# Half of a batch's feed-forward moved out of the attention stage, by way of DRAM, into Strassen's form

## The chip, the cores and the metric

The kernel runs on one core of one Trainium2 chip. Its engines are TensorE (PE in the profile; PEld is its weight load), VectorE (DVE), ScalarE (ACT), GpSimd (POOL) and SyncE (SP), which issues most of the DMAs. The metric is the device time in microseconds (us). Each engine works its own list of instructions, which is fixed when the program is built; a layer that plans the program sets the order in each list.

## The reference

Four batches of eight heads with 768 positions and a head dimension of 64. Queries and keys are each given to the nearest of 16 centroids of their head; a query sees the keys of its own cluster alone. The heads' results stand side by side as 3072 rows of 512 features, and these go through a feed-forward block: a product with `w_in` (512 x 2048), the square of the positive part, and a product with `w_out` (2048 x 512).

```python
q_assign = np.argmax(np.einsum('bhsd,hcd->bhsc', q_n, c_n), axis=-1)   # q_n, k_n, c_n: of length 1
k_assign = np.argmax(np.einsum('bhsd,hcd->bhsc', k_n, c_n), axis=-1)
mask = q_assign[:, :, :, None] == k_assign[:, :, None, :]
scores = np.where(mask, scale * np.matmul(q, k.transpose(0, 1, 3, 2)), -1000000000.0)
attn = np.exp(scores - np.max(scores, axis=-1, keepdims=True))
attn = attn / (np.sum(attn, axis=-1, keepdims=True) + 1e-09)
x = np.matmul(attn, v).transpose(0, 2, 1, 3).reshape(B * S, H * D)
r = np.maximum(x @ w_in, 0.0)
out = (r * r) @ w_out
```

The weights come as 64-bit numbers, which the kernel rounds to 32 bits itself.

## The kernel before

**Units.** Attention goes by pairs of heads (16 pairs, four to a batch) and by halves `h` of the 768 queries (384 columns, `TB`). One unit is one pair, one half and 256 of the 768 keys: 96 units, numbered 0 to 95 here; batch 0 has units 0 to 23, and each later pair has six units, three for `h` = 0 and three for `h` = 1.

**One unit of batches 1 to 3.** `scores` puts four products (two chunks of keys, two heads) into two PSUM tiles named `sc`, chunk 1 first. There are two such tiles (`ps_sc`), so the next unit's scores write the same two again. ScalarE takes the exponential in place, one instruction for each tile (line 466). VectorE reads the PSUM tile, sets to zero what belongs to another cluster, and writes an SBUF tile `ex` (line 470, four instructions a unit, here called masks; two for each `sc` tile). A tile of scores is free only when its two masks are done. `times_v` multiplies `ex` by the values two units later (`LAG = 2`), into `av`. GpSimd adds the `ex` tiles up for the sums (lines 480 and 482). In batch 0 the mask is part of the product instead, and ScalarE writes `ex` itself.

**The end of a half.** Three units after its first scores, the sums are spread by a product with ones (`sm`), VectorE takes the reciprocal `r` (line 551), which goes by SyncE to DRAM (`far_r`) and comes back to all partitions (`rb`); VectorE multiplies `av` by it into `xT` (line 570).

**The next pair.** Its queries and keys are turned by DMA (`qkT<-words`), multiplied by the centroids (`lg`), copied (`lgs`), transposed (`lt`), and VectorE finds the clusters in five instructions (`number`: `mx`, `best` twice, `ids`, `ids_b`). These numbers are turned (`pb`), copied (`row`), and go by way of DRAM to all partitions (`qid`).

**The fill.** Between these products TensorE works on the feed-forward of batch 0, in plain form: a generator `ffn(b, h)` yields after each product, and the loop over units takes as many columns from it as `density` and what is `left` ask for. `ffn` first makes 16 tiles `gT`, one for each 128 of the 2048 features (`ph`, line 584: 4 products of 384 columns each; ScalarE then does lines 591 and 592), and then three times 16 products of 512 columns (`po`, line 597). The fill uses the PSUM pool `ps_f` of two banks together with `sm`, `lg`, `lt` and `pb`.

**After attention.** For batches 1, 2, 3 in turn `ffn_pair` does the feed-forward in Strassen's form, with 7 products where the plain form has 8: first up (line 676, all of `g`, 16 x 2 x 384 columns for each partition), then down (line 707), in three column parts `i` of 128. `combine` adds the seven results up on VectorE (line 646 and `sub`, line 618). `w_sums` are the four sums of blocks of `w_out` (tiles `w_t`) that the down products need; they are made once.

A product of 32-bit numbers shows in the profile as two MATMUL records, so a unit has 8 records of `sc` and 8 of `av`.

Of the kernel before, what the change touches and what calls it, by code (L numbers as in the profile page):

```python
# [8 lines left out]
F32 = mybir.dt.float32  # L9
# [16 lines left out]
def kernel(  # L26
# [28 lines left out]

    outer, ctx, keep, early = ctx, ExitStack(), ExitStack(), ExitStack()
    xtp = keep.enter_context(tc.tile_pool(name="xtp", bufs=1))
    gtp = ctx.enter_context(tc.tile_pool(name="gtp", bufs=FT))
    xt_first = ctx.enter_context(tc.tile_pool(name="xt_first", bufs=1))
    loads = ctx.enter_context(tc.tile_pool(name="loads", bufs=4))  # L60
    loads_v = ctx.enter_context(tc.tile_pool(name="loads_v", bufs=2))
# [11 lines left out]
    once_early = early.enter_context(tc.tile_pool(name="once_early", bufs=1, side="right"))  # L73
    later = {}

    dram = ctx.enter_context(tc.tile_pool(name="dram", bufs=2, space=bass.MemoryType.DRAM))
    ps_sc = ctx.enter_context(tc.tile_pool(name="ps_sc", bufs=2, space=PSUM))
    ps_av = ctx.enter_context(tc.tile_pool(name="ps_av", bufs=2, space=PSUM))
# [496 lines left out]


    out_view = out.rearrange("(b p j) m -> b j p m", p=P, j=NCH)

    def ffn(b, h):
        gT = []  # L580
        for f in range(FT):
            ph = bank("ph", [P, TB])
            for kk in range(KT):
                nc.tensor.matmul(  # L584
                    ph, lhsT=w_in[:, kk, f * P : (f + 1) * P], rhs=xT[b, h][:, kk],
                    start=(kk == 0), stop=(kk == KT - 1),
                )
                if kk < KT - 1:
                    yield TB
            gT.append(gtp.tile([P, TB], F32, name="gT"))  # L590
            nc.scalar.activation(out=gT[f], in_=ph, func=ACT.Relu)
            nc.scalar.square(gT[f], gT[f])
            yield TB
        for i in range(NB):
            po = bank("po", [P, DM])
            for f in range(FT):
                nc.tensor.matmul(  # L597
                    po, lhsT=gT[f][:, i * P : (i + 1) * P], rhs=w_out[:, f],
                    start=(f == 0), stop=(f == FT - 1),
                )  # L600
                if f < FT - 1:
                    yield DM
            osb = later["out"].tile([P, DM], F32, name="osb")
            nc.scalar.copy(out=osb, in_=po)
            nc.sync.dma_start(out_view[b, h * NB + i], osb)
            yield DM

    def ffn_pair(pools, b):  # L610

        gp, sp, tp, bk = pools
        H2, F2, M2 = KT // 2, FT // 2, DM // 2
        x = [[xT[b, h][:, H2 * g : H2 * (g + 1)] for h in range(2)] for g in range(2)]
        t1, t2, t4 = (tp.tile([P, H2, TB], F32, name=f"x_t{i}") for i in (1, 2, 4))

        def sub(out, a, b, eng=nc.vector):
            eng.tensor_tensor(out=out, in0=a, in1=b, op=ALU.subtract)

        with tc.issue_after(last_exp[0]):  # L620
            sub(t1, x[0][1], x[0][0])
            sub(t2, x[1][1], t1)
            sub(t4, t2, x[1][0])
            sub(x[0][1], x[1][1], x[0][1])
        t3 = x[0][1]
        g = gp.tile([P, FT, 2, TB], F32, name="g")

        def combine(c, product, width, early=()):

            (c11, c12), (c21, c22) = c

            waiting = {}

            def bank_of(j):
                if j in waiting:
                    return waiting[j]
                bank = bk(width)
                product(j, bank)  # L640
                return bank

            def add(j, *results):
                bank = bank_of(j)
                for out, to in results:
                    nc.vector.tensor_tensor(out=out, in0=bank, in1=to, op=ALU.add)  # L646

            bank = bk(width)
            product(1, bank)
            nc.scalar.copy(out=c11, in_=bank)  # L650
            for j in early:
                waiting[j] = bank_of(j)
            add(6, (c12, c11))
            add(2, (c11, c11))
            add(7, (c21, c12))
            add(5, (c22, c21), (c12, c12))
            sub(c21, c21, bank_of(4))
            add(3, (c12, c12))

        for i in range(F2):  # L660
            lo, hi = slice(i * P, (i + 1) * P), slice((F2 + i) * P, (F2 + i + 1) * P)
            a = [[w_in[:, H2 * g2 : H2 * (g2 + 1), cols] for g2 in range(2)] for cols in (lo, hi)]
            w_s = sp.tile([P, 4, H2, P], F32, name="w_s", tag=f"s{i % 2 + 1}")
            s1, s2, s3, s4 = (w_s[:, j] for j in range(4))
            nc.gpsimd.tensor_tensor(out=s1, in0=a[1][0], in1=a[1][1], op=ALU.add)  # L665
            sub(s2, s1, a[0][0], nc.gpsimd)
            sub(s3, a[0][0], a[1][0], nc.gpsimd)
            sub(s4, a[0][1], s2, nc.gpsimd)
            operands = {
                1: (a[0][0], x[0][0]), 2: (a[0][1], x[1][0]), 3: (s4, x[1][1]), 4: (a[1][1], t4),  # L670
                5: (s1, t1), 6: (s2, t2), 7: (s3, t3),
            }

            def product(j, bank):
                for kk in range(H2):
                    nc.tensor.matmul(  # L676
                        bank, lhsT=operands[j][0][:, kk], rhs=operands[j][1][:, kk],
                        start=(kk == 0), stop=(kk == H2 - 1),
                    )

            if i > 1 and w_sums:
                to, one, two = w_sums.pop(0)
                sub(w_t[to], one, two)
            c = [[g[:, f, h] for h in range(2)] for f in (i, F2 + i)]
            combine(c, product, TB)
            nc.scalar.activation(out=c[0][0], in_=c[0][0], func=ACT.Relu)
            nc.scalar.square(c[0][0], c[0][0])
            for to in (c[1][1], c[1][0], c[0][1]):
                nc.vector.scalar_tensor_tensor(
                    out=to, in0=to, scalar=0.0, in1=to, op0=ALU.max, op1=ALU.mult  # L690
                )

        for i in range(NB):
            cols = slice(i * P, (i + 1) * P)
            a = [[g[:, F2 * g2 : F2 * (g2 + 1), h, cols] for g2 in range(2)] for h in range(2)]
            s1, s2 = (sp.tile([P, F2, P], F32, name=f"g_s{j}", tag=f"s{j}") for j in (1, 2))
            nc.vector.tensor_tensor(out=s1, in0=a[1][0], in1=a[1][1], op=ALU.add)
            sub(s2, s1, a[0][0])
            sub(a[1][0], a[0][0], a[1][0])
            operands = {  # L700
                1: (a[0][0], w_q[0][0]), 2: (a[0][1], w_q[1][0]), 3: (a[0][1], w_q[1][1]),
                4: (a[1][1], w_t[4]), 5: (s1, w_t[1]), 6: (s2, w_t[2]), 7: (a[1][0], w_t[3]),
            }

            def product(j, bank):
                for f in range(F2):
                    nc.tensor.matmul(  # L707
                        bank, lhsT=operands[j][0][:, f], rhs=operands[j][1][:, f],
                        start=(f == 0), stop=(f == F2 - 1),
                    )  # L710
                if j == 2:
                    sub(a[0][1], a[0][1], s2)

            osb = [later["out"].tile([P, DM], F32, name="osb") for _ in range(2)]
            c = [[osb[h][:, M2 * m : M2 * (m + 1)] for m in range(2)] for h in range(2)]
            last = b == B - 1 and i == NB - 1
            combine(c, product, M2, early=(2, 4))

            for h in (1, 0):
                for cols in (slice(0, M2), slice(M2, DM)) if last and h == 0 else (slice(0, DM),):  # L720
                    nc.sync.dma_start(out_view[b, h * NB + i][:, cols], osb[h][:, cols])


# [5 lines left out]
        for pair in pairs for h in halves for c in range(0, NCH, 2)  # L729
    ]  # L730
    LAG = 2
    per_half = FT * KT * TB + NB * FT * DM
    PLAIN = [(0, 0), (0, 1)]
    fill = []
    left = [len(PLAIN) * per_half]
    RESERVE = 3 * DM

    ENDS = len(units) + LAG

    def density(u):  # L740


        return 4 if u < HP * NCH else 2 if u < len(units) - NCH else 3

    def fill_steps(columns):

# [34 lines left out]
    for u in range(len(units) + LAG + 2):  # L781
# [59 lines left out]
        for pair, h in now + [d for d in [added.pop(0)] if d]:  # L841
# [3 lines left out]
            if hp == HP - 1 and (h == 1 or b == 0):  # L845
                for half in [(b, h)] if b == 0 else [(b, 0), (b, 1)]:
                    if half in PLAIN:
                        fill.append(ffn(*half))

    flag = const.tile([P, 1], I32, name="flag")  # L850

    def check_sums():
# [21 lines left out]
        fast.enter_context(tc.tile_pool(name=name, bufs=1, reuse_waits="tile"))  # L874
        for name in ("wtp", "tp", "sp", "gp")
    )
    pools = gp, sp, tp, lambda width: banks.tile([P, width], F32, name="bank", tag="bank")
    w_q = [
        [w_out[:, FT // 2 * g : FT // 2 * (g + 1), DM // 2 * m : DM // 2 * (m + 1)] for m in range(2)]
        for g in range(2)  # L880
# [1 line left out]
    w_t = {i: wtp.tile([P, FT // 2, DM // 2], F32, name=f"w_t{i}") for i in range(1, 5)}  # L882
    w_sums = [(1, w_q[0][1], w_q[0][0]), (2, w_q[1][1], w_t[1]), (3, w_q[1][1], w_q[0][1]),
              (4, w_t[2], w_q[1][0])]
    for b in range(B):
        if (b, 0) not in PLAIN:
            ffn_pair(pools, b)
            if w_sums is not None:
                w_sums = None
                check_sums()  # L890
                again = nc.values_load(flag[0:1, 0:1], min_val=0, max_val=1)
    fast.close()
    keep.close()

# [189 lines left out]
```

## Time and profile before

| | |
|---|---|
| Time, median of 3 | 996.61 us (996.1 to 996.9) |
| Span of the profiled execution | 993.0 us |
| Granted TensorE clock, mean | 0.998 |
| TensorE busy | 976.9 us, 98% |
| VectorE, GpSimd, ScalarE busy | 567.6, 376.6, 316.3 us |
| `ph`, records and busy time | 256, 96.2 us |
| `po`, records and busy time | 192, 99.4 us |
| First product after attention | at 552.6 us |

A busy time is a union of records, and the end of a matmul's record is modelled; the time from one product to the next, read from the chain of waits or the timeline, says what a product costs in its place. The stage of attention and the stage of Strassen's form have different limits, so they are read separately.

### The profile page before, as it was taken

Reading aid. Unit: us, or ns where it says so; the run is one execution under the profiler, and the core shown is the slowest. Engines: PE = TensorE matmul, PEld = TensorE weight load, DVE = VectorE, ACT = ScalarE, POOL = GpSimd, SP = SyncE. Lnnn points to the kernel's source line nnn. Section 1 sums busy time; section 2 is a strip of 40 time slices with the busy share of each in tenths; the row PEclk is TensorE's granted clock in tenths of the full one; section 3 lists DMA queues with packets and bytes.
Section 4 is the critical chain, followed back from the end, with each engine's and each line's share of the span. In section 5 each row is a group of like instructions: output and inputs, shape, how many; then the busy total and the mean of one; then the engine's idle time right before and its main releaser. Section 6 shows DMA issues by size and latency. Waiting matters only on the chain.

```text
span 993.0 us, 12061 instructions
## 1 busy us (share of the span) xinstructions
PE 976.9 (98%) x4455; PEld 543.9 (55%) x4455; DVE 567.6 (57%) x913; ACT 316.3 (32%) x510; POOL 376.6 (38%) x277
## 2 busy tenths in 40 slices
PE   8999999999999999999999999999999999999997
PEld 4544443333334444433333555888655888556886
DVE  4779766666565555665765766533465531556331
ACT  5887665443434554444233111000111000111000
POOL 1238665655555555556466442001331002231000
PEclk9999999999999999999999999999999999999999
DMA  9655764445444444444210000000000000000000
GB/s 258 182 187 170 212 171 109 91 120 128 115 112 115 107 114 108 100 117 115 66 55 12 28 0 1 1 22 22 21 1 1 11 22 24 10 0 1 22 22 25
DMA packets 127576, 74.33 MB, mean 75 GB/s; under 512 B 90906, under 2 KB 118934, under 8 KB 127510
## 3 DMA queue, kind: packets, MB, share of 16 engines
q1 hardware_dynamic: 125798, 73.06, 27.6%
q8 instruction: 37, 0.61, 0.3%
q10 hardware_dynamic: 1712, 0.43, 0.2%
q14 instruction: 29, 0.24, 0.1%
HBM read 48.07 MB, written 15.86 MB: 64 GB/s over the span
## 4 chain that ended last, share of the span: by engine, by line
PE 91%; DVE 3%; DMA 1%; issue 1%; ACT 1%; SPq 1%; POOL 0%; ACTq 0%; DVEq 0%; POOLq 0%
PE bank L707 22%; PE bank L676 22%; PE po L597 9%; PE ph L584 8%; PE sc L91 7%; PE av L91 7%; PE sc L94 7%; PE av L94 6%; PE sm L94 1%; PE sm L91 1%; DVE ex L470 1%; PE lg L91 1%; PE lt L317 1%; DMA rb<-far_r 1%; DMA k_raw<-in_k_dram 1%
## 5 line engine op out<-in xcount | busy, mean ns | idle before, releaser
L482 POOL TENSOR_TENSOR acc<-acc,ex 128x768 f32<-128x768 f32 x112 | 205.2, 1832 | 114.2 <-DVE ex L470 101.2
L470 DVE SCALAR_TENSOR_TENSOR ex<-qid,ids,sc 128x384 f32<-128x384 bf16 x288 | 158.6, 606 | 68.3 <-ACT sc L466 58.5
L466 ACT ACTIVATE sc<-sc 128x768 f32<-128x768 f32 x144 | 108.4, 793 | 148.2 <-PE sc L94 131.2
L94 PE MATMUL sc<-qkT 64*128 64x384 f32 x576 | 151.7, 504 | 0.5
L94 PE MATMUL av<-ex,v_raw 128*64 128x384 f32 x576 | 144.4, 494 | 0.0
L646 DVE TENSOR_TENSOR g<-bank,g 128x384 f32<-128x384 f32 x144 | 77.8, 555 | 79.9 <-PE bank L676 78.6
L665 POOL TENSOR_TENSOR w_s<-w_in 128x256 f32<-128x256 f32 x24 | 18.5, 769 | 275.7 <-PE bank L707 162.0
L597 PE MATMUL po<-w_out,gT 128*128 128x512 f32 x192 | 99.4, 626 | 0.0
L584 PE MATMUL ph<-xT,w_in 128*128 128x384 f32 x256 | 96.2, 506 | 0.6 <-DVE r L551 0.6
L707 PE MATMUL bank<-w_out,g 128*128 128x256 f32 x432 | 95.2, 379 | 0.0
L91 PE MATMUL sc<-qkT 64*128 64x384 f32 x192 | 87.7, 537 | 3.1 <-DVE ex L470 3.0
L707 PEld LDWEIGHTS bank<-w_out,g 128*128 128x128 f32 x432 | 82.1, 190 | 11.8
L646 DVE TENSOR_TENSOR osb<-bank,osb 128x256 f32<-128x256 f32 x54 | 22.1, 423 | 107.6 <-PE bank L707 102.2
L91 PE MATMUL av<-ex,v_raw 128*64 128x384 f32 x192 | 82.5, 512 | 0.3 <-DVE xT L570 0.3
L94 PEld LDWEIGHTS sc<-qkT 64*128 64x128 f32 x576 | 65.2, 187 | 27.6 <-issue 4.8
L480 POOL TENSOR_TENSOR acc<-ex 128x768 f32<-128x768 f32 x28 | 52.5, 1876 | 60.0 <-DVE ex L470 57.9
L584 PEld LDWEIGHTS ph<-xT,w_in 128*128 128x128 f32 x256 | 44.3, 189 | 46.9 <-issue 20.1
L676 PE MATMUL bank<-xT,w_in 128*128 128x384 f32 x192 | 69.8, 487 | 0.0
L676 PE MATMUL bank<-x_t,w_s 128*128 128x384 f32 x192 | 69.7, 486 | 0.0
L676 PE MATMUL bank<-xT,w_s 128*128 128x384 f32 x192 | 69.7, 486 | 0.0
L551 DVE RECIPROCAL r<-sm 128x192 f32<-128x192 f32 x31 | 42.0, 1355 | 44.9 <-PE sm L94 44.9
L707 PE MATMUL bank<-w_t,g 128*128 128x256 f32 x288 | 65.1, 379 | 0.0
(128 smaller groups left out, 1226.2 us busy)
## 6 DMA issues: line engine op xcount, KB each, us to landing
words<-flat SPq DMA_DIRECT2D x24, 384.0 KB
w_raw<-in_moe_w_in_dram SPq DMA_DIRECT2D x16, 512.0 KB
w_raw<-in_moe_w_out_dram SPq DMA_DIRECT2D x16, 512.0 KB
v_raw<-in_v_dram SPq DMA_DIRECT2D x20, 384.0 KB
q_raw<-in_q_dram SPq DMA_DIRECT2D x31, 192.0 KB
k_raw<-in_k_dram SPq DMA_DIRECT2D x31, 192.0 KB
rb<-far_r SPq DMA_DIRECT2D x62, 96.0 KB
out_dram<-osb SPq DMA_DIRECT2D x23, 256.0 KB
```

Of the source, the lines that this page charges most:

```text
L91: last = nc.tensor.matmul(**next(products))
L94: last = nc.tensor.matmul(**product)
L466: last_exp[0] = nc.scalar.activation(out=t[:, 2 * i : 2 * i + 2] if pair < HP else src, in_=src, func=ACT.Exp, scale=SCALE).ins
L470: nc.vector.scalar_tensor_tensor(out=t[:, 2 * i + e], in0=qid[pair][1][:, h, e], scalar=ids[pair][:, ch % NB, 2 + ch // NB, e : e + 1], in ...
L480: nc.gpsimd.tensor_tensor(out=acc[pair, h], in0=t[:, 0:2], in1=t[:, 2:4], op=ALU.add)
L482: nc.gpsimd.tensor_tensor(out=acc[pair, h], in0=acc[pair, h], in1=t[:, 2 * i : 2 * i + 2], op=ALU.add)
L551: nc.vector.reciprocal(out=r, in_=sm)
L584: nc.tensor.matmul(ph, lhsT=w_in[:, kk, f * P : (f + 1) * P], rhs=xT[b, h][:, kk], start=(kk == 0), stop=(kk == KT - 1),)
L597: nc.tensor.matmul(po, lhsT=gT[f][:, i * P : (i + 1) * P], rhs=w_out[:, f], start=(f == 0), stop=(f == FT - 1),)
L646: nc.vector.tensor_tensor(out=out, in0=bank, in1=to, op=ALU.add)
L676: nc.tensor.matmul(bank, lhsT=operands[j][0][:, kk], rhs=operands[j][1][:, kk], start=(kk == 0), stop=(kk == H2 - 1),)
L707: nc.tensor.matmul(bank, lhsT=operands[j][0][:, f], rhs=operands[j][1][:, f], start=(f == 0), stop=(f == F2 - 1),)
```

## The change

Only the up part of batch 0's feed-forward stays in attention as fill. Each `gT` tile is written to a DRAM tile `g_far` as soon as it is squared, so four `gT` buffers do where 16 were needed. After batch 1's down part has used a column part of `g`, that part is loaded with batch 0's squares, and `down_pair(0, g)` runs between batch 1's down part and batch 2's up part, in seven products instead of eight. `ffn_pair` is split into `up_pair` and `down_pair`, `combine` and `sub` move out of it as they are, and the amount of fill (`per_half`), what is kept for the end (`RESERVE`) and `density` are set anew. What it is for: TensorE does an eighth less work in that product.

```diff
-    gtp = ctx.enter_context(tc.tile_pool(name="gtp", bufs=FT))
+    gtp = ctx.enter_context(tc.tile_pool(name="gtp", bufs=4))
...
+    far = outer.enter_context(tc.tile_pool(name="far", bufs=1, space=bass.MemoryType.DRAM))
...
-    def ffn(b, h):
-        gT = []
+    g_far = far.tile([P, FT, 2, TB], F32, name="g_far")
+
+    def ffn_up(b, h):
         for f in range(FT):
...
-            gT.append(gtp.tile([P, TB], F32, name="gT"))
-            nc.scalar.activation(out=gT[f], in_=ph, func=ACT.Relu)
-            nc.scalar.square(gT[f], gT[f])
+            gT = gtp.tile([P, TB], F32, name="gT")
+            nc.scalar.activation(out=gT, in_=ph, func=ACT.Relu)
+            nc.scalar.square(gT, gT)
+            nc.sync.dma_start(g_far[:, f, h], gT)
             yield TB
-        for i in range(NB):
-            po = bank("po", [P, DM])
-            for f in range(FT):
-                nc.tensor.matmul(
-                    po, lhsT=gT[f][:, i * P : (i + 1) * P], rhs=w_out[:, f],
-                    start=(f == 0), stop=(f == FT - 1),
-                )
-                if f < FT - 1:
-                    yield DM
-            osb = later["out"].tile([P, DM], F32, name="osb")
-            nc.scalar.copy(out=osb, in_=po)
-            nc.sync.dma_start(out_view[b, h * NB + i], osb)
-            yield DM
...
-    per_half = FT * KT * TB + NB * FT * DM
+    per_half = FT * KT * TB
...
-    RESERVE = 3 * DM
+    RESERVE = 4 * TB
...
-        return 4 if u < HP * NCH else 2 if u < len(units) - NCH else 3
+        return 6 if u < HP * NCH else 2 if u < len(units) - NCH else 3
...
-    for b in range(B):
-        if (b, 0) not in PLAIN:
-            ffn_pair(pools, b)
-            if w_sums is not None:
-                w_sums = None
-                check_sums()
-                again = nc.values_load(flag[0:1, 0:1], min_val=0, max_val=1)
+    for b in range(1, B):
+        up_pair(b, g)
+        w_sums = None
+        if b == 1:
+            check_sums()
+            again = nc.values_load(flag[0:1, 0:1], min_val=0, max_val=1)
+        down_pair(b, g, b == B - 1)
+        if b == 1:
+
+            for i in range(NB):
+                cols = slice(i * P, (i + 1) * P)
+                nc.sync.dma_start(g[:, :, :, cols], g_far[:, :, :, cols])
+            down_pair(0, g)
```

## The prediction, made before the changed kernel ran

> **What bounds the kernel now.** I read the page's shares and slices first, then the chain of waits, which gives the cost of products in their place, then the timeline of a few units of attention.
>
> ```profile
> PE 976.9 (98%) x4455; PEld 543.9 (55%) x4455; DVE 567.6 (57%) x913; ACT 316.3 (32%) x510; POOL 376.6 (38%) x277
> PE   8999999999999999999999999999999999999997
> PE 91%; DVE 3%; DMA 1%; issue 1%; ACT 1%; SPq 1%; POOL 0%; ACTq 0%; DVEq 0%; POOLq 0%
> ...
> 85.21 4.07 PE ph L584 x12
> 181.25 1.91 PE po L597 x4
> 320.74 2.13 PE ph L584 x6
> 549.95 2.77 PE po L597 x6
> 552.73 72.24 PE bank L676 x224
> 624.97 72.52 PE bank L707 x336
> ```
>
> TensorE is never idle, and it makes up 91% of the chain. From the chain's pieces: `ph` costs 0.32 us a record and 0.19 for changing over (12 records 4.07, 6 records 2.13), `po` 0.43 a record and the same 0.19 (6 records 2.77, 4 records 1.91). One batch's down part in Strassen's form is 336 records in 72.5 us. So TensorE is the limit; how far the others are behind shows only inside a unit. VectorE's row and TensorE's row around units 36 to 38, then unit 43:
>
> ```profile
> 225.60 1.36 DVE L551 RECIPROCAL r<-sm 128x192 f32<-128x192 f32 x1 [1.35 <-PE sm L94]
> 227.36 2.19 DVE L470 SCALAR_TENSOR_TENSOR ex<-qid,ids,sc 128x384 f32<-128x384 bf16 x4 [0.40 <-ACT sc L466]
> 232.03 0.56 DVE L570 SCALAR_TENSOR_TENSOR xT<-av,rb 128x384 f32<-128x384 f32 x1 [2.48 <-DMA rb<-far_r]
> 232.51 2.18 DVE L470 SCALAR_TENSOR_TENSOR ex<-qid,ids,sc 128x384 f32<-128x384 bf16 x4
> ...
> 225.47 0.59 PE L91 MATMUL sc<-qkT 64*128 64x384 f32 x1
> 226.96 0.54 PE L91 MATMUL av<-ex,v_raw 128*64 128x384 f32 x1
> 228.40 1.98 PE L597 MATMUL po<-w_out,gT 128*128 128x512 f32 x4
> 230.31 0.59 PE L91 MATMUL sc<-qkT 64*128 64x384 f32 x1
> ...
> 266.25 0.56 DVE L570 SCALAR_TENSOR_TENSOR xT<-av,rb 128x384 f32<-128x384 f32 x1 [4.83 <-DMA rb<-far_r]
> 266.72 2.18 DVE L470 SCALAR_TENSOR_TENSOR ex<-qid,ids,sc 128x384 f32<-128x384 bf16 x4
> 268.00 0.56 PE L91 MATMUL sc<-qkT 64*128 64x384 f32 x1 [0.90 <-DVE ex L470]
> ```
>
> See three things. A plain unit is 4.84 us: scores 1.49, `av` 1.44, fill 1.91. Its masks start 1.9 after the scores and take 0.55 each, so the two `sc` tiles are free at 3.0 and 4.1; the next scores, of which the second half starts 0.75 after the first, could start 3.5 after these. The slack is 1.35 us, and the fill is what makes it. And unit 43: `xT` stood in VectorE's list ahead of the masks, `rb` came late, and TensorE waited 0.9; it went on 0.2 after the first two masks. `rb` takes 6.4 us from the start of `r` (225.60 to 232.03).
>
> **What the Trainium skill says.** "Perfetto Trace Analysis", section Engine Utilization, calls matmul busy time a bad metric, since matmuls are pipelined; the trace agrees: `po` is 192 records in 99.4 us busy, 0.52 each, but 0.43 in the chain. "TensorE: Matmul & The Clock Gate", section Specifications, gives ScalarE and VectorE strictly ordered queues of 8; agrees: in unit 43 masks whose scores were long there stood behind an `xT` that waited. "DMA: Bandwidth & Descriptors", section Anatomy of one DMA, gives some 2 us fixed for each DMA (for the other issuing path); `far_r` and `rb` are two in a row with issues and `r` around them, 6.4 in this trace.
>
> **The change part by part.** The walk below uses the lists of the built program, which are fixed.
>
> *The down part added.* 336 records as in batch 1: 72.5 us. The loads of `g` hide: SyncE issues the first behind the first column part of batch 1's down part, some 40 us before VectorE wants it, and each is 2.1 MB; even at 100 GB/s (slices of attention ran 91 to 212) that is 21 us. 0.3 for the added boundary: +72.8.
>
> *Batch 0, units 14 to 23.* The fill goes from 6 `ph` to 4: 4 records of 0.32, -1.3 a unit, -12.9. VectorE is busy 64.8 of 82.8 us there (windows 75.4 to 158.2, weights being rounded); in 69.9 that is 93%, and unit 24 already began its masks 3.4 late behind that work. I keep -10.5. Units 24 and 25 wait for this VectorE work, 26 to 29 lose 0.4 each: -2.
>
> *Ten pairs, units 30 to 89.* The fill goes from 2 `po` a unit (1.91) to 1 `ph` (0.84). Lists of one pair, M = mask:
>
> ```
> TensorE before   38 sc av po lg po sm | 39 sc lt av po po | 40 sc av po pb po | 41 sc av po po sm | 42, 43 sc av po po
> TensorE after    38 sc av ph lg | 39 sc sm av ph lt | 40 sc av ph pb | 41 sc av ph sm | 42, 43 sc av ph
> VectorE before   r M39 M39 mx M39 best M39 best ids ids_b xT M40 x4, M41 x4, r M42 x4, xT M43 x4
> VectorE after    M39 M39 r M39 M39 mx best best M40 ids M40 ids_b M40 M40 xT M41 x4, r M42 x4, M43 xT M43 x3
> ```
>
> By TensorE alone the units are 4.6, 4.8, 4.0, 4.25, 3.8, 3.8, 25.2 for a pair (`sm` 0.47, `lg` 0.78, `lt` 0.53, `pb` 0.2); before, 6.3, 5.4, 5.2, 5.3, 4.85, 4.85, 31.9. Now VectorE, from unit 39's scores at 0: two masks 1.9 to 3.0, `r` to 4.36, two masks to 5.5, `mx`, `best`, `best` (0.55, 0.55, 0.67) to 7.2. `lt` waits for the bank that `r` read, so unit 40's scores start at 4.95. Its masks, ready at 6.85, stand behind and between the clusters' work: M, `ids`, M, `ids_b`, M, M to 10.55. Unit 41's second half of scores needs the last of them, so unit 41 starts at 9.95: unit 40 takes 5.0, not 4.0. Unit 41 is covered (4.25). Unit 42 starts at 14.2, `r` at 14.35, unit 43 at 18.0. `rb` is there 6.4 after `r`, at 20.8, or 0.5 later where the `qkT` transpose, which held SyncE 2.6 to 4.4 us for each issue, is in front; three of unit 43's masks stand behind `xT` (in every second pair all four), and it takes 4.4 to 5.4, say 4.9. Sum 4.6 + 4.95 + 5.0 + 4.25 + 3.8 + 4.9 = 27.5. Units 30 to 89 took 193.6 to 516.1, 322.5 us; ten pairs at 27.5 are 275: -47.5, where TensorE alone would give -71.
>
> *Other edits of attention.* The writes of `g_far` (0.2 MB) stand on SyncE's queue among the `r` and `rb` issues and wait for ScalarE's square; that comes before `r` is ready, so an issue of 0.5 us is the cost, inside the range taken for `rb`. Four `gT` buffers cover 10 units or more. ScalarE is at 2.5 us of a unit, GpSimd at 3.1: not in the way.
>
> *Last units and the passage.* Units 90 to 95 and the last fill: -2.5. Then a new wait. Before, VectorE's list was `xT w_t w_t xT w_t w_t g`: two of the `w_t` (2.6 each) ran while `rb` was on its way, and the additions into `g` began 10.4 us after the first product (562.96 against 552.56), just when the 8 banks at 1.29 us were full. After, it is `xT xT w_t w_t w_t g w_t g`. From unit 95's start: first product at 12, the last `xT` near 20 (the second `r` stands behind the first `xT`, then 6.4 for `rb`), three `w_t`, one addition, the fourth `w_t`, and the first of the adding banks is free at 30.8, when TensorE has been out of banks since 23.6. +7 (4 to 8).
>
> Sum: 996.6 + 72.8 - 10.5 - 2 - 47.5 - 2.5 + 7 = 1014.
>
> **The rivals.** (a) TensorE stays the only limit: -12.9 - 3.4 - 71 - 2.5 + 72.8 and no stop at the passage, 980. For it: no unit but 24, 25, 43 and 82 waited before. Against: the lists put 8.6 us of VectorE work in a row across units 39 and 40, and the slack is 0.3 where it was 1.35. (b) Only part of the waits comes: `rb` faster by 1 us, or the two `best` overlapping better; 12 less in the pairs and 3 less at the passage: 999. For it: `rb` took between 5.7 and 6.8. (c) More waits: `qid` comes too late for the next pair's first mask (7 us from `pb` to it, where it was 8.4), or batch 0 gains nothing: +10, 1024. (d) The loads of `g` come late and stop TensorE for one of them: +20, 1034; against it, the 24 us between the parts.
>
> **How the numbers follow.** The forecast 0.57, (a) 0.1, (b) 0.18, (c) 0.12, (d) 0.03. The prediction is 1014. Ends of the unknown terms: `rb` plus or minus 0.5 in ten pairs, 5; the passage, 3; batch 0, 3. Leaving out (a), (d) and the far side of (c), the range is 993 to 1024. Faster takes (a) and a little of (b), 0.13; same 0.05; slower 0.82.
>
> **What would show it.** Right: in the changed kernel six units of a pair take near 27.5 us, with TensorE idle before `sc` behind masks in unit 41 and after 43, 2 us a pair; VectorE's masks of unit 40 end 5.6 after its scores; TensorE stops some 7 us after its first nine products behind attention; 336 more `bank` records in 72.5 us with no stop ahead of them. Wrong: pairs near 25, or a stop at `g<-g_far`.

## The result and the profile after

The changed kernel takes 1036.01 us (median of 4, 1033.64 to 1043.69) where the kernel before took 996.75 in the same series: a ratio, of the means, of 1.0408, 95% interval 1.0353 to 1.0463, 4% slower. The direction was as forecast; the time is 22 us above the forecast, 1014, and 12 beyond the upper end of the range.

From the page of the changed kernel (busy times; TensorE's busy slices and its granted clock in 40 slices; the chain of waits by engine):

```profile
span 1035.3 us, 12468 instructions
...
PE 983.6 (95%) x4599; PEld 576.3 (56%) x4599; DVE 596.3 (58%) x946; ACT 316.6 (31%) x507; POOL 384.3 (37%) x277
...
PE   8999979988998888889989999999999999999997
...
PEclk9999989999999999999999999999999999999999
...
PE 71%; DVE 11%; DMA 7%; issue 4%; ACT 3%; POOL 2%; SPq 1%; ACTq 0%; DVEq 0%; POOLq 0%
```

TensorE was 91% of the chain before and is 71% now; what came in is VectorE, DMA and "issue". But for the first and the last slice, the seven and the eights of its row lie in slices 6 to 21: batch 0, the pairs and the passage behind them. The next two views are the busy time in five stretches (start and end, length, then busy time and records of PE, PEld, DVE, ACT, POOL, then the granted clock, the DMA share and GB/s): units 14 to 23, 24 to 29, the ten pairs of units 30 to 89, units 90 to the first product after attention, and the rest. First the kernel before, then the changed one:

```profile
81.90:158.20 76.30, 75.37 (x354) 35.13 (x352) 58.36 (x53) 50.88 (x87) 54.01 (x33) 1.00 0.66 181
158.20:193.60 35.40, 33.62 (x158) 12.87 (x155) 23.56 (x37) 14.84 (x22) 19.61 (x12) 1.00 0.37 88
193.60:516.10 322.50, 320.16 (x1518) 123.97 (x1514) 198.25 (x334) 141.89 (x213) 181.55 (x100) 1.00 0.42 106
516.10:552.60 36.50, 36.50 (x171) 13.64 (x168) 19.91 (x31) 8.99 (x12) 26.23 (x19) 1.00 0.07 24
552.60:993.20 440.60, 434.72 (x1683) 318.98 (x1681) 211.53 (x355) 40.38 (x82) 70.01 (x90) 1.00 0.04 13
```

```profile
81.90:154.70 72.80, 66.59 (x318) 29.90 (x316) 62.01 (x54) 46.19 (x77) 56.48 (x33) 0.95 0.77 212
154.70:187.80 33.10, 31.23 (x149) 12.06 (x148) 23.50 (x38) 15.81 (x25) 18.54 (x12) 0.95 0.44 119
187.80:483.30 295.50, 266.86 (x1366) 98.77 (x1362) 194.34 (x330) 140.68 (x207) 180.57 (x100) 0.97 0.50 122
483.30:518.50 35.20, 34.32 (x173) 13.89 (x170) 25.84 (x34) 12.54 (x20) 26.44 (x16) 1.00 0.13 41
518.50:1035.30 516.80, 507.78 (x2019) 382.68 (x2017) 234.62 (x390) 41.96 (x86) 76.75 (x94) 1.00 0.09 26
```

Attention gave back 3.5 us in units 14 to 23, 2.3 in the next six, 27.0 in the pairs and 1.3 in the last ones; the second stage grew by 76.4 (993.0 less 552.6 is 440.4 before). TensorE's idle time in the pairs went from 2.3 us to 28.6. And the clock is no longer 1.00 in the first three stretches.

Where the idle time in the pairs is, the start of each unit's scores in the timeline tells. Lengths of six units, us, worked out from those starts, for four of the ten pairs (unit 0 is the first of a pair's six, so the units 38 to 43 of the walk stand here as 2, 3, 4, 5, 0, 1):

```
               unit 0  unit 1  unit 2  unit 3  unit 4  unit 5    sum
walked          3.8     4.9     4.6     4.95    5.0     4.25    27.5
units 30-35     3.77    4.72    4.96    4.85    4.59    4.56    27.45
units 36-41     3.77    5.96    4.96    4.85    4.59    4.56    28.69
units 42-47     3.77    6.51    6.24    4.85    4.60    4.56    30.53
units 66-71     3.77    6.66    6.46    4.85    4.60    4.56    30.90
```

The first unit and the last three are the same in every pair (but for unit 75, 5.2): the first takes 3.77 as walked, the last three 14.0 together where 14.2 was walked. The second is longer in every pair but the first, by 0.6 to 1.8 us, and the third takes 4.96 or, in six pairs, 6.2 to 6.6. For one such pair, the timeline of the changed kernel (start, us, engine, line, instruction; in brackets the idle time before it and what ended that):

```profile
391.39 4.70 SPq L289 DMA_TRANSPOSE qkT<-words  x1
...
393.93 1.36 DVE L552 RECIPROCAL r<-sm 128x192 f32<-128x192 f32 x1 [0.60 <-PE sm L95]
...
396.15 0.53 SPq L555 DMA_DIRECT2D far_r<-r  x1
...
398.24 1.13 SPq L559 DMA_DIRECT2D rb<-far_r  x2
...
401.92 0.56 DVE L571 SCALAR_TENSOR_TENSOR xT<-av,rb 128x384 f32<-128x384 f32 x1 [4.04 <-DMA rb<-far_r]
...
402.39 2.18 DVE L471 SCALAR_TENSOR_TENSOR ex<-qid,ids,sc 128x384 f32<-128x384 bf16 x4
...
403.67 0.56 PE L92 MATMUL sc<-qkT 64*128 64x384 f32 x1 [2.26 <-DVE ex L471]
```

`r` is done at 395.29, but SyncE is in the issue of the transpose until 396.09, so `far_r` starts 2.22 us after the start of `r`, `rb` another 2.1 later, and `xT` 8.0 after `r`. Masks stand behind `xT`, and TensorE waits 2.26 us. The same place of the kernel before, SyncE's own queue, with `r` at 225.60:

```profile
221.76 3.61 SPq L288 DMA_TRANSPOSE qkT<-words  x1
226.99 0.54 SPq L554 DMA_DIRECT2D far_r<-r  x1
...
228.62 1.12 SPq L558 DMA_DIRECT2D rb<-far_r  x2
```

There the transpose ended 0.23 us before `r` began, and `far_r` followed 1.39 after the start of `r`. In the pairs of the changed kernel from unit 36 on, the transpose starts some 2.6 us before `r`, where it had been 2.3 to 4.9 and mostly 3.8: with shorter units `r` comes sooner behind it. And its issue takes 4.3 to 5.2 us there, where it took 2.6 to 4.4; what made it longer was not tried. Over the changed kernel `far_r` comes 1.39 after `r` in unit 30, where the transpose ended 0.3 after the start of `r`; 1.8 to 3.3 in units 36, 42 and so on to 84, where it ended 1.7 to 2.6 after it; and 1.37 to 1.39 in the other halves from unit 24 on.

The kernel before has this collision once among its pairs, with the `r` at the start of unit 42:

```profile
255.18 4.38 SPq L288 DMA_TRANSPOSE qkT<-words  x1
...
257.47 1.36 DVE L551 RECIPROCAL r<-sm 128x192 f32<-128x192 f32 x1 [1.35 <-PE sm L94]
...
260.24 0.55 SPq L554 DMA_DIRECT2D far_r<-r  x1
...
262.83 1.12 SPq L558 DMA_DIRECT2D rb<-far_r  x2
```

The transpose ended 2.09 us after the start of `r`, `far_r` came 2.77 after it and `xT`, at 266.25, 8.8 after it. This is the late `rb` of unit 43 that the prediction shows, with TensorE's wait of 0.9 behind it.

The third unit's loss is something else. Three stretches of 3.41 us one after the other, around the start of unit 44 (columns as above):

```profile
251.29:254.70 3.41, 0.75 (x4) 0.33 (x4) 1.63 (x4) 0.00 (x0) 0.00 (x0) 0.99 0.97 251
254.70:258.11 3.41, 3.41 (x12) 1.06 (x10) 1.83 (x4) 1.82 (x3) 2.69 (x2) 0.51 0.61 141
258.11:261.52 3.41, 3.41 (x22) 1.28 (x20) 0.94 (x2) 1.72 (x3) 3.18 (x3) 1.00 0.36 98
```

TensorE waited 2.66 us in the first; in the second, with work all the time, its granted clock is 0.51 and it does 12 records where the third has 22. The pairs have six such stretches, always in the unit after a late `xT`, where it costs 1.3 to 1.65 us.

Units 14 to 23 lost most of their gain in one unit, unit 21, which takes 14.8 us (9.3 before). The timeline there, TensorE's sums and the transpose `lt`, VectorE between them (lines 156 to 163 round the weights):

```profile
126.25 0.33 PE L92 MATMUL sm<-acc,ups 128*32 128x192 f32 x1
...
127.74 1.39 DVE L160 TENSOR_SCALAR w_out<-w_out 128x512 uint32<-128x512 uint32 x1
...
129.06 2.31 DVE L163 SCALAR_TENSOR_TENSOR w_raw<-w_raw 128x512 uint32<-128x512 uint32 x1
...
131.29 2.02 DVE L156 TENSOR_SCALAR w_out<-w_out 128x512 f32<-128x512 f32 x1
...
133.23 1.77 DVE L163 SCALAR_TENSOR_TENSOR w_raw<-w_raw 128x512 uint32<-128x512 uint32 x1
...
135.25 1.35 DVE L552 RECIPROCAL r<-sm 128x192 f32<-128x192 f32 x1
...
136.65 0.90 PE L318 MATMUL lt<-ident,lgs 128*128 128x128 f32 x3 [5.96 <-DVE r L552]
```

The sums `sm` were ready near 126.6; `r` ran 8.7 us later, behind the rounding. `sm` holds a bank of the pool that `lt` needs, so TensorE waited 5.96 us for `r`, and from 135.2 on its clock is at half for 6.8.

The second stage, from the chain of waits (start, us, line, records):

```profile
518.66 9.04 PE bank L663 x28
...
535.10 59.58 PE bank L663 x184
594.80 145.24 PE bank L695 x672
```

The two down parts run as one piece, 672 records in 145.24 us, 72.6 each: nothing waits for the loads of `g`. The first up part takes 76.1 from 518.66 to 594.80 and 72.24 in the later batches: the passage costs 3.9, of which the timeline shows 2.0 as a wait for VectorE's additions into `g` and 1.3 for GpSimd's `w_s`.

### The profile page after: what moved, and what is told of

It reads as the page before. It is cut to its first block, busy times and chain, and to the rows that moved or that the text cites. A ratio compares the mean times of both kernels' runs of the same rounds, so it can differ in the third digit from the quotient of the medians.

```text
span 1035.3 us, 12468 instructions
## 1 busy us (share of the span) xinstructions
PE 983.6 (95%) x4599; PEld 576.3 (56%) x4599; DVE 596.3 (58%) x946; ACT 316.6 (31%) x507; POOL 384.3 (37%) x277
## 4 chain that ended last, share of the span: by engine, by line
PE 71%; DVE 11%; DMA 7%; issue 4%; ACT 3%; POOL 2%; SPq 1%; ACTq 0%; DVEq 0%; POOLq 0%
PE bank L695 28%; PE bank L663 21%; PE sc L95 5%; PE sc L92 5%; DVE ex L471 4%; PE ph L585 4%; PE av L92 3%; DMA rb<-far_r 3%; PE av L95 3%; DMA far_r<-r 2%; DVE r L552 2%; POOL acc L483 2%; DVE w_raw L163 2%; DVE w_out L156 1%; PE sm L95 1%
## 5 line engine op out<-in xcount | busy, mean ns | idle before, releaser
L95 PE MATMUL sc<-qkT 64*128 64x384 f32 x576 | 161.1, 525 | 2.0
L95 PE MATMUL av<-ex,v_raw 128*64 128x384 f32 x576 | 151.6, 513 | 0.0
L695 PE MATMUL bank<-w_out,g 128*128 128x256 f32 x576 | 126.9, 379 | 0.0
L695 PEld LDWEIGHTS bank<-w_out,g 128*128 128x128 f32 x576 | 109.4, 190 | 15.3
L623 DVE TENSOR_TENSOR osb<-bank,osb 128x256 f32<-128x256 f32 x72 | 29.5, 423 | 141.8 <-PE bank L695 136.3
L585 PE MATMUL ph<-xT,w_in 128*128 128x384 f32 x256 | 109.1, 532 | 0.0
L92 PE MATMUL sc<-qkT 64*128 64x384 f32 x192 | 88.4, 541 | 21.6 <-DVE ex L471 21.6
L92 PE MATMUL av<-ex,v_raw 128*64 128x384 f32 x192 | 87.1, 537 | 0.2 <-DVE xT L571 0.2
L695 PE MATMUL bank<-w_t,g_s 128*128 128x256 f32 x384 | 86.8, 379 | 0.0
L695 PE MATMUL bank<-w_t,g 128*128 128x256 f32 x384 | 86.8, 379 | 0.0
L695 PEld LDWEIGHTS bank<-w_t,g 128*128 128x128 f32 x384 | 73.0, 190 | 9.9
L695 PEld LDWEIGHTS bank<-w_t,g_s 128*128 128x128 f32 x384 | 73.0, 190 | 9.9
```

Of the source, the lines that this page charges most:

```text
L92: last = nc.tensor.matmul(**next(products))
L95: last = nc.tensor.matmul(**product)
L585: nc.tensor.matmul(ph, lhsT=w_in[:, kk, f * P : (f + 1) * P], rhs=xT[b, h][:, kk], start=(kk == 0), stop=(kk == KT - 1),)
L695: nc.tensor.matmul(bank, lhsT=operands[j][0][:, f], rhs=operands[j][1][:, f], start=(f == 0), stop=(f == F2 - 1),)
```

## The experiments

The kernel before ran beside every group of runs; its median was 993.4 to 994.5 there. Runs are compared by these ratios. The single steps from e3 to e10 are 2 to 4 us each, with an uncertainty of 4 us for the first and of some 2 us for the others, so for these steps the traces carry the reading; from e3 to e10 together it is 11 us, with 4 of uncertainty.

| run | us, median | ratio to before, 95% interval |
|---|---|---|
| e1_no_down | 957.52 | 0.9632 (0.9583 to 0.9681) |
| e2_no_far | 954.79 | 0.9579 (0.9536 to 0.9622) |
| e3_later | 1002.49 | 1.0089 (1.0056 to 1.0123) |
| e4_zeros | 1026.34 | 1.0311 (1.0276 to 1.0345) |
| e5_turn_later | 1034.09 | 1.0397 (1.0363 to 1.0431) |
| e8_turn_behind_rb | 1013.69 | 1.0196 (1.0175 to 1.0217) |
| e6_r_first | 999.43 | 1.0052 (1.0035 to 1.0068) |
| e7_w_t_last | 994.79 | 1.0019 (1.0003 to 1.0035) |
| e9_all | 993.12 | 0.9996 (0.9987 to 1.0004) |
| e10_slow_rounding | 991.18 | 0.9977 (0.9964 to 0.9990) |

**e1_no_down: what the added down part costs.** The second product of batch 0 is left out.

```diff
-            for i in range(NB):
-                cols = slice(i * P, (i + 1) * P)
-                nc.sync.dma_start(g[:, :, :, cols], g_far[:, :, :, cols])
-            down_pair(0, g)
```

> Left out: the loads of g and the down part of batch 0, so batch 0's rows of the result are not written; its squares still go to DRAM. Theory (the down part costs its 336 records and nothing else; the loss lies in attention): 1036 - 72.8 = 963, 959 to 967. Rival (loads or the added boundary stop TensorE as well): below 957. Attention keeps its pauses and its stretches of half clock in both.

957.52 lies between the theory's range and the rival's bound, and alone decides for neither. The difference in ratio to the changed kernel, 0.078, is 77 us, with some 7 us of uncertainty, where the chain has 72.6 for the part itself. And 0.9632 is a gain of 37 us from attention and the passage, where the sum had 55: what is missing is missing there, not in the down part.

**e2_no_far: are the writes of squares in the way of `rb`?** As e1, and `g_far` is not written.

```diff
-            nc.sync.dma_start(g_far[:, f, h], gT)
```

> Left out, beside what e1_no_down leaves out: the 32 writes of the squares to DRAM. Theory (rb is late because the transpose of qkT holds SyncE's queue, the writes matter little): within 4 of e1_no_down, 958 to 965. Rival (the writes on SyncE's queue and on the DMA engines are what makes rb late, and so the pauses and the half clock): at least 12 less than e1_no_down, 951 or below.

2.7 us less than e1, inside the spread of both and far from the 12 of the rival. In the halves with a transpose in front its issue still took 3.9 to 5.0 us and `xT` came 7 to 8.2 us after `r`. The writes are not the cause, or a small part of it.

**e3_later: `xT` one unit later on VectorE**, behind the masks of the next unit, so that no mask waits for `rb`. (`tc.issue_after(x)` orders what stands in it behind `x` in its engine's list; `last_mask` is the last mask.)

```diff
...
-    added = [None]
-    for u in range(len(units) + LAG + 2):
+    added = [None, None]
+    for u in range(len(units) + LAG + 3):
...
-            with tc.high_priority(offset=1000) if wide(pair, h) else ExitStack():
+            with (tc.high_priority(offset=1000) if wide(pair, h)
+                  else tc.issue_after(last_mask[0]) if last_mask[0] else ExitStack()):
```

> xT is put one unit later in VectorE's list, behind the masks of the unit that waited for it; nothing else moves. Theory (the masks stand behind xT, xT waits for rb, TensorE pauses, and a pause of this length is followed by a stretch of half clock): the unit falls from 5.5 to 6.6 to 3.8, the half clock in units 44 to 80 goes, ten pairs get 2.0 + 1.0 shorter, 1036 - 30 = 1006, 1001 to 1012. Rival (VectorE's work as such, or GpSimd, is the limit of a pair, and the wait only comes up elsewhere): not under 1025.

1002.49, inside the theory's range. The six units took 3.77, 3.77, 4.56, 4.85, 4.59 and 4.56 in nearly every pair, 26.1 together, and units 30 to 89 took 262.0 us at a clock of 1.00, though `far_r` was as late as in the changed kernel, 1.5 to 3.0 us after `r`. So a late `rb` costs only through what stands behind `xT`, and with that wait the half clock in the pairs goes too. Unit 21 was about as long as in the changed kernel, 14.6 us.

**e4_zeros: is it the pause that halves the clock?** Three products with weights of zero, which change no sum, go into the fill of units 31, 37 and so on to 85. They give TensorE some 19 us of extra work (six records of 0.32 us in each of ten pairs), which lies where the pause was.

```diff
...
+    zeros = const.tile([P, P], F32, name="zeros")
+    nc.gpsimd.memset(zeros, 0.0)
+    extra = [0]
...
+                idle = [zeros] * extra[0]
+                extra[0] = 0
+                ops = ops + idle if kk == 0 else idle + ops
...
+        if 30 <= u < 90 and u % 6 == 1:
+            extra[0] = 3
```

> Three products with zeros for weights (1.95 us) are added to the fill of each of the ten units that wait for rb; the result is the same. Theory (half clock follows a pause, and these units have 1.7 to 2.8 us of it): the units stay at their length, the half clock in units 44 to 80 goes, the time falls by 5 to 12, 1024 to 1031. Rival (the half clock has another cause, or TensorE's work still counts there): 1036 to 1056.

1026.34, as expected: ten us less with more work. The wait of `sc` for masks in the table of waits (us in total, times, longest), changed kernel, then e4_zeros:

```profile
PE sc L92 <- DVE ex L471: 21.6, 11, 2.8
```

```profile
PE sc L92 <- DVE ex L471: 4.2, 8, 1.7
```

The 1.7 lies ahead of the pairs; in them no wait is longer than 0.7 us now, the pairs have no half clock, and the third unit takes 4.96 at most; the second still takes 5.7 to 6.5, since `xT` is as late. That separates the two losses: the half clock comes from the pause, the pause from the lateness.

**e5_turn_later and e8_turn_behind_rb: the transpose out of the way of `far_r`.** The first moved the call one unit down in the program:

```diff
-            lambda: turn_words(pair), None, first, None, None, None,
+            None, None, first, lambda: turn_words(pair), None, None,
```

> The changed kernel with one edit: the DMA transpose qkT of the next pair is issued one unit later, so SyncE is not held by it when r's copy to DRAM (far_r) is due. Same work, same order on TensorE and VectorE. Theory (the factors r come back late because far_r waits behind the transpose on SyncE): in the halves that start at units 36, 42, ... rb lands 6.4 to 6.9 us after r instead of 7.5 to 9.1, unit 37 takes 4.4 to 4.95 us instead of 5.5 to 6.7, the stop on the masks falls under 1.7 us and with it the stretches at half clock in the pairs; a pair takes 26.5 to 28, and the whole 1009 to 1021 us. Rival (the path r, far_r, rb is late for the traffic on the DMA engines, or the transpose only moves its delay to the other half's rb or to the scores that read qkT): rb stays over 7.4 in one of the two halves and the time stays at 1028 us or more.

The time, 1034.09, is that of the changed kernel. It says nothing on the theory: in the trace the transpose stands where it stood, ahead of `far_r` and 2.6 us before `r`, and every engine has the same instructions in the same order as in the changed kernel, since the planner sets the order. So this run is the changed kernel once more. The second run keeps that edit and orders the transpose behind the last `rb`:

```diff
     def turn_words(pair):
         qkT[pair] = qktp.tile([P, 2 * NCH, P], F32, name="qkT")
-        nc.sync.dma_start(
+        with tc.issue_after(last_rb[0]):
+            nc.sync.dma_start(
...
-                nc.sync.dma_start(rb[D * e : D * (e + 1)], far[e].partition_broadcast(D))
+                last_rb[0] = nc.sync.dma_start(rb[D * e : D * (e + 1)], far[e].partition_broadcast(D)).ins
```

> The changed kernel with the transpose qkT of the next pair ordered behind the copies rb on SyncE (in e5_turn_later the planner had put it back to where it was, so nothing was moved there). TensorE's order is the same; on VectorE four of the pairs have xT one mask earlier. Theory (far_r waits on SyncE behind the transpose's 2.6 to 4.7 us): rb of the halves that start at units 36, 42, ... lands 6.3 to 6.9 us after r, as it does in unit 30, where no transpose was in front; unit 37 then takes about the 4.7 us of unit 30's neighbour 31, the pauses of over 1.75 us and the half clock are gone from the pairs, a pair takes 27.5 us as in units 30 to 35, and the whole 1036 less nine times 2.0 to 2.3 us: 1013 to 1020 us. Rival (rb is late for another cause, or the transpose, now later, makes the logits lg of unit 38 wait): rb over 7.4 or a new stop at lg, and 1028 us or more.

1013.69, inside the theory's range. The pair of unit 42, which took 30.53 in the changed kernel, in the timeline of this one:

```profile
237.08 1.36 DVE L554 RECIPROCAL r<-sm 128x192 f32<-128x192 f32 x1 [0.32 <-PE sm L95]
...
238.47 0.53 SPq L557 DMA_DIRECT2D far_r<-r  x1
...
240.09 1.12 SPq L561 DMA_DIRECT2D rb<-far_r  x2
...
241.31 3.22 SPq L290 DMA_TRANSPOSE qkT<-words  x1
...
243.97 0.56 DVE L573 SCALAR_TENSOR_TENSOR xT<-av,rb 128x384 f32<-128x384 f32 x1 [2.99 <-DMA rb<-far_r]
...
245.72 0.56 PE L92 MATMUL sc<-qkT 64*128 64x384 f32 x1 [1.15 <-DVE ex L473]
```

`far_r` comes 1.39 after `r` and `rb` is issued 3.01 after it, and so in every pair. TensorE waits 1.15 here and 2.3 at most, the pairs have no half clock, and units 30 to 89 take 277.1 us, 18.3 less. In four pairs `xT` also stands one mask earlier in VectorE's list, which puts more masks behind it and can hardly have helped. So most of both losses in the pairs comes from SyncE being in the transpose. What is left, `xT` 6.4 to 8.0 us after `r` where 6.3 to 6.9 was expected, is the landing of `rb`; what makes that vary was not tried.

**e6_r_first: unit 21.** As e3, and the rounding of units 20 and 21 goes behind `r` on VectorE.

```diff
...
-        while rounding >= 3:
+        while rounding >= 3 and u != 20:
...
-                with tc.issue_after(last_exp[0]):
+                with tc.issue_after(last_exp[0]), tc.issue_after(last_r[0]) if u == 21 else ExitStack():
```

> The kernel of e3_later (xT one unit later) with one more edit: the rounding operations of units 20 and 21 are put behind the reciprocal r of the half that ends there on VectorE. Theory (unit 21 is long because r stands behind about five rounding operations, the bank of sm is not freed, the routing's transpose lt waits for that bank, and the pause then halves TensorE's clock): unit 21 takes 7 to 9 us instead of 14.6, its stretch at half clock is gone, and the time is 5 to 8 us below e3_later, 994 to 998 us. Rival (VectorE is full there and the rounding only moves the wait to the next units or to the routing's sums): units 20 to 25 take as long as in e3_later together, 48 us, and the time stays within 2 us of it.

999.43, by ratio 3.7 us below e3, where 5 to 8 were expected. From the timeline:

```profile
128.43 0.33 PE L92 MATMUL sm<-acc,ups 128*32 128x192 f32 x1
...
128.85 1.36 DVE L554 RECIPROCAL r<-sm 128x192 f32<-128x192 f32 x1 [0.28 <-PE sm L95]
...
133.56 0.49 PE L318 MATMUL lt<-ident,lgs 128*128 128x128 f32 x3
```

`r` follows the sums at once, `lt` waits for nothing, and the unit takes 6.4 us. But units 22 and 23 take 7.9 and 9.6 instead of 7.1 and 6.7: TensorE waits 2.8 us for an `xT` there and has 3.4 us of half clock after it. Part of the wait was mended, and the rest came back two units later, as the rival had it for all of it. Units 20 to 25 take 44.6 us, 46.9 in e3.

**e7_w_t_last: the passage.** As e6, with the sums `w_t` ordered behind the additions of the group before.

```diff
...
                 to, one, two = w_sums.pop(0)
-                sub(w_t[to], one, two)
+                with tc.issue_after(added_up[0]):
+                    sub(w_t[to], one, two)
```

> The kernel of e6_r_first with one more edit: in the first half of the feed-forward behind attention the sums of weight blocks w_t are put behind the additions of the group before them on VectorE. Theory (the stop of some 4 us in the passage is TensorE waiting for a bank or operand that VectorE gives late because w_t stands ahead of it): the stop of 2.0 us on VectorE's additions is gone, 2 to 4 us less than e6_r_first. Rival (the stop is the feed-forward's own start, w_s on GpSimd and x_t on VectorE): the time is within 1 us of e6_r_first.

994.79, by ratio 3.3 us less, as expected. The chain of waits has the first up part in one piece, so the wait for GpSimd's `w_s` went as well: beside `w_t` two of its operations had taken 2.77 us each, and here they take 1.04 and 0.72.

```profile
481.05 72.24 PE bank L666 x224
553.41 145.24 PE bank L699 x672
```

**e9_all and e10_slow_rounding: the rest of batch 0.** In e7 the transpose stood in front of `rb` there too:

```profile
135.63 3.53 SPq L289 DMA_TRANSPOSE qkT<-words  x1
...
139.26 1.18 SPq L562 DMA_DIRECT2D rb<-far_r  x2
...
143.45 0.56 DVE L574 SCALAR_TENSOR_TENSOR xT<-av,rb 128x384 f32<-128x384 f32 x1 [4.58 <-DMA rb<-far_r]
...
144.06 0.54 PE L92 MATMUL av<-ex,v_raw 128*64 128x384 f32 x1 [2.87 <-DVE xT L574]
```

e9 adds e8's edit to e7; e10 adds to e9 one number, the rate at which weights are rounded:

```diff
-        rounding += 4
+        rounding += 4 if u < 16 else 3
```

> The kernel of e7_w_t_last with the transpose qkT ordered behind rb. The orders of TensorE and VectorE are the same. Theory: in e7_w_t_last the pairs have no stop left (26.1 us), so nothing is gained there; but in units 22 and 23 rb waits behind a transpose of 3.5 us, xT is late, TensorE pauses for 2.9 us and then has half its clock for 3.4 us; with that gone 3 to 6 us less, 989 to 992 us, 0.2 to 0.5% faster than the kernel before. Rival (the weight loads or the rounding on VectorE set these units anyway): within 1.5 us of e7_w_t_last.

> The kernel of e9_all with the weight rounding spread further: from unit 16 on three units' share instead of four is added per unit, so that one block is rounded per unit and the last one some five units later. Theory (what is left to stop TensorE in units 20 to 29 of e9_all is VectorE, where rounding operations of up to 2.3 us stand ahead of the masks; its one stop there is 3.9 us and the half clock after it): units 18 to 29 take 69 to 71 us instead of 74.8, and the time is 3 to 6 us below e9_all, 987 to 990 us, 0.3 to 0.6% faster than the kernel before. Rival (the loads of the weights, or the rounding wherever it goes, hold the masks as long): within 1.5 us of e9_all.

e9 took 993.12, by ratio 2.3 us less than e7 and short of the 3 to 6 expected: the pause on `xT` is gone, but unit 24 now waits 3.9 us for masks that stand behind rounding, and half clock follows. e10 took 991.18: no half clock is left in attention behind unit 0, and the total gained another 1.9, where 3 to 6 were expected, since units 18 to 29 take 72.4 us and not 69 to 71. e10 is 0.23% faster than the kernel before, which its interval, 0.9964 to 0.9990, just separates from no change. With its waits mended, the change takes 76.0 us out of attention (first product behind it at 476.5, 552.6 before), little more than the 72.6 that it puts behind it.

## Why the prediction was wrong

On the profiled runs the prediction was 993.0 + 17.4 = 1010.4, and the span is 1035.3: 24.9 us to account for.

| step of the sum | predicted | measured | off |
|---|---|---|---|
| down part added | +72.8 | +72.6 | 0 |
| batch 0, units 14 to 23 | -10.5 | -3.5 | +7.0 |
| units 24 to 29 | -2 | -2.3 | -0.3 |
| ten pairs | -47.5 | -27.0 | +20.5 |
| last units and last fill | -2.5 | -1.3 | +1.2 |
| passage | +7 | +3.9 | -3.1 |

*The down part* held, and so did the claim that the loads hide; rival (d) falls.

*The ten pairs: the step that failed.* The walk put `rb` "6.4 after `r`, at 20.8, or 0.5 later where the `qkT` transpose, which held SyncE 2.6 to 4.4 us for each issue, is in front". The transpose was named, and its hold was known, but its place was not walked. In units 10 to 22% shorter than before (5.38 to 4.85, 4.85 to 3.77) it starts some 2.6 us before `r` and, with a longer issue, ends 1.7 to 2.6 after the start of `r`, where in nine of the ten pairs before it ended 2.3 before to 0.5 after. So `xT` came 7.5 to 9.1 after `r`: the "0.5 later" was 1.1 to 2.7. The pair of unit 42 in the kernel before showed it, with 8.8; "`rb` took between 5.7 and 6.8", in rival (b), leaves it out. The lateness made the second unit 5.8 instead of 4.9 on average, some 9 us over ten pairs. With the transpose out of the way (e8) the pairs take 277.1 where 275 was walked.

*Around the clusters' work* the sum was right in part by luck: the three units took 14.0 us where 14.2 was walked, but not as walked. TensorE did not wait before unit 41's scores; it waited 0.6 a pair at `pb` for `ids_b`, and unit 40 took 4.6, not 5.0, unit 41 4.6, not 4.25. Rival (a), TensorE alone, was 25.2 a pair where e3, without the wait on `xT`, shows 26.1.

*What was missing from the sum:* that a pause of some 2 us costs a second time. Six of ten pairs had a stretch of half clock, 1.3 to 1.65 us each, some 9 us in all. e4 shows that this is tied to the pause: less pause, more work, and no half clock. The rest of the 20.5 is the third unit's 4.96 where 4.6 was walked, 3.6 in ten pairs (4.56 in e3, so this too goes with `xT`), less some 2 won in the others. No rival had a half clock in it. Rival (d)'s 1034 is near the measured time by chance; its stop is not there.

*Batch 0.* "I keep -10.5" came from a mean, VectorE at 93%. The mean hid an order: `r` stood behind rounding operations, and `lt` behind `r`, for the one free bank. In the changed kernel rival (c)'s "batch 0 gains nothing" was nearer than the forecast. But the gain was there to have: units 14 to 29 took 111.7 us before, 99.2 was forecast, and they take 106.0 in the changed kernel, 102.0 in e6, 99.7 in e9 and 97.2 in e10. So it was the order in VectorE's and SyncE's lists, with the rate of the rounding, that kept it away, and not the 93% as such.

*The passage* was mis-sized, 7 against 3.9: TensorE stopped 9.0 us after the first product, where the walk had 11.6, and then only in short pauses. e7 shows that the named cause, `w_t` ahead of the additions, was the right one; that it also slowed GpSimd's `w_s` was not in the walk.

*The whole.* Slower, which had 0.82, was right. That the sum came out at 1014 and e8 at 1013.69 is no proof of each term: in e8 batch 0's units 14 to 23 took 68.7 against 65.8, and the passage 6.1 against 7, with half clock in it.

## What to carry to other kernels

When work is taken out of a loop, what is left of it runs sooner, but a trip through DRAM and the issue of a long DMA do not get shorter with it (here the issue of the transpose grew): place each of them anew against the shorter loop, on the queue that issues it, before counting the gain. Look first whether the kernel before has the collision somewhere already. A wait that TensorE takes alone is not the whole price; if it lasts about 2 us, add what half clock costs in the stretch after it. And an order written in the program is only an order if the planner must keep it: look at the list of the engine after each edit.

## What the runs showed of the hardware

*Half clock after a short pause.* The starts of the stretches at half clock lie multiples of 3.413 us apart. In the changed kernel, of the windows of that grid, those of attention with 1.77 to 3.41 us of TensorE idle, eight in number, were all followed by one at half clock; three with 1.24, 1.37 and 1.56 us idle were not. The Trainium skill, "TensorE: Matmul & The Clock Gate", section What's actually happening, has the free-running window of 3413 ns, which the trace bears out, and has the half rate after one or more idle windows of about 3.4 us; its section HAM oscillation asks for no gaps over that. Here about half of a window was enough. It is no sharp rule: in other runs windows with 1.68 (e7) and 1.70 us (e2) were followed by half clock, and at the start of the changed kernel one with 1.61; not followed were 1.72 in e8, 1.86 in e7, and at the passage 1.84 in e4 and, in two pieces, 1.86 in the changed kernel. The edge lies somewhere between 1.6 and 1.9 us here.

*VectorE beside GpSimd.* The rounding operation of line 160 took 0.42 us at 120.72, with GpSimd idle, and 1.39 at 127.74 beside it; that of line 163 0.69 at 121.06 and 2.31 at 129.06. The Trainium skill, "GPSIMD Engine Reference", section 1. Specifications, says that the two share their SBUF interfaces, with contention for VectorE instructions with two SBUF inputs or in a two-port mode. The trace agrees for line 163, which has two inputs, with a factor of 3.3 at these sizes; line 160 has one input and the same factor, and its mode is not shown here.
